# A two-layer convolution and feed-forward kernel: first h in two halves, new instruction orders, some PSUM copies on the other engine

## The chip, the cores and the metric

The kernel runs on one core of a Trainium2 chip. Five engines work side by side, each through its own queue in order: TensorE (PE, matrix products and transposes), VectorE (DVE), ScalarE (ACT), GpSimd (POOL) and SyncE (SP, which here only issues DMA transfers). PE writes to PSUM, and DVE or ACT has to copy a result from there to SBUF before PE can use it again. The metric is the device time of one execution in microseconds, lower is better, given as the median of several runs.

## What is computed

Two layers of the same two steps run over a sequence of 2048 rows of 512 channels in bfloat16. Step A is a long convolution (a short 4-tap convolution of k, times v, then convolved with a filter as long as the sequence, times the normalised input), step B a gated feed-forward block with 1792 hidden channels:

```python
def _A_ref(q, k, v, shift_k, ssm_k, ssm_D):
    ...
    for t in range(ks):
        k_shift = k_shift + k_pad[:, t:t + S, :] * shift_k[:, ks - 1 - t][None, None, :]
    kv = k_shift * v
    ...
    y = y + kv * ssm_D[None, None, :]      # y: kv convolved with ssm_k along the sequence
    return q * y

def _B_ref(x, w_gate, w_up, w_down):
    g = _silu(x @ w_gate)
    u = x @ w_up
    return (g * u) @ w_down

x = A_q
x = x + _A_ref(_layernorm(x, axis=-1), A_k, A_v, A_shift_k, A_ssm_k, A_ssm_D)
x = x + _B_ref(_layernorm(x, axis=-1), B_w_gate, B_w_up, B_w_down)
x = x + _A_ref(_layernorm(x, axis=-1), A_k, A_v, A_shift_k, A_ssm_k, A_ssm_D)
x = x + _B_ref(_layernorm(x, axis=-1), B_w_gate, B_w_up, B_w_down)
```

The convolution result y depends on k, v and the filter alone, so it is the same in both layers and is computed once.

## The kernel before

**Tiling.** The sequence is cut into four blocks c = 0..3 of 512 rows, a block into four residues r of 128 rows. The long convolution is done block by block in a spectrum: the filter's block (h, 512 channels by 512 positions, which has to be turned so that positions lie on partitions) and the block of kv go through small Fourier matrices (`fwd`), are multiplied on DVE (`product`, L665 to L679; block 0 in the form at L654 and L658) and come back through `inv`. Block 0 has its own code at the front; blocks 1 to 3 are spread among the feed-forward work.

**Units.** The feed-forward work comes in 16 units (layer, block, half), in the order block by block, in a block layer 0 half 0, layer 0 half 1, layer 1 half 0, layer 1 half 1. Before a unit, `prologue` takes the statistics of its two rows (bn_stats L821, bn_aggr L822, ve L824; or on ACT, L840 to L853), raises variance plus epsilon to the power -1/2 on POOL (`rstd`, L826 or L855: the power step), normalises (n or z, L879 on DVE, L874 on ACT), and, for the feed-forward input, turns z into zT with two DMA transposes on SP (L908). The first unit's z is turned on PE instead and copied from PSUM at L938 and L940. `gate_up` multiplies zT by the gate and up weights (PSUM tiles `pf`), ACT takes the silu of the one (sg, L974) and copies the other (ht, L977), DVE multiplies the two (L979); `down` multiplies ht by the last weights (PSUM tiles `pd`), ACT copies them (dn, L1075) and DVE adds them to x (L1078).

**The front.** SP issues h, k, v and q of block 0, then h and v of block 1 and the weights. PE turns h (`transpose_h`, L489, 16 transposes of 128 by 128, four to a residue), DVE or ACT copies them to hs (L499, L505; residue 0 with an addition, L502), PE multiplies by `fwd`, and the results are copied (`evacuate`, ev) and summed to G (L457, L459). `fwd` is made by DVE (index arithmetic `ph`), ACT (sine, L1145) and DVE again (the sign flips, L1151). k is turned on PE and copied to kTb (L384, L386); 16 diagonal matrices `dg` are built from the four taps (L1188, L1192) for the short convolution on PE (L522), whose result DVE multiplies by v (L536). Until the first h is there PE runs products of ones (`warm`, L1307), whose number `Plan.issue` works out from the planned starts.

**The order.** Every instruction is an entry of a list, made in program order by `plan.add` with its engine, a planned cost and what it reads and writes. The table ORDER (L55 to L113) holds for each entry its place in one global sequence; each engine's queue is that sequence cut down to the engine. The planned costs do not change the order: `Plan.order` uses them to choose which buffer of a ring a tile gets, and `issue` for the warming products. PW and PWA are the planned costs of the power step after DVE and ACT statistics.

Of the kernel before, what the change touches and what calls it, by code (L numbers as in the profile page):

```python
# [23 lines left out]
PW = 1.2  # L24
# [18 lines left out]
H_SPLIT = False  # L43
PWA = 2.4
EVEN = True
SUMS = False
K0 = "rows"
CK0, LT0 = 3.0, 3.5
# [5 lines left out]
SHARE = {(1, 0, 1): 2, (0, 2, 0): 2, (1, 3, 0): 2}  # L54
ORDER = [  # L55
# [57 lines left out]
]  # L113
R = 4
NZ = 3
# [1225 lines left out]
```

## Time and profile before

| | us |
|---|---|
| median of 3 runs (lowest, highest) | 343.08 (342.94, 343.32) |
| span of the profiled execution | 341.1 |
| PE busy | 336.9 (99%) |
| DVE busy | 282.4 (83%) |
| ACT busy | 252.5 (74%) |
| POOL busy | 37.3 (11%) |
| PE in the chain that ended last | 94% of the span |

The profile is one execution; its span runs from the first to the last instruction, and the runs' times contain what lies around the span. Busy shares are averages over stages: DVE and ACT are nearly full in the first hundred microseconds and have room at the end, so a stage's own row says more than the total. Rows in order of time give start, duration, engine, line, operation, written tile and what it reads, then in brackets the idle time of the engine before and what ended it; rows that name several instructions run together what follows closely on its engine. PE's products overlap: the next one starts before the former has left the array.

### The profile page before, as it was taken

To read this page: it belongs to the slowest core of one execution; us is meant where nothing else is said; L and a number is where in the kernel's file an instruction comes from. 1 tells how busy PE (TensorE), PEld (TensorE's weight loads), DVE (VectorE), ACT (ScalarE), POOL (GpSimd) and SP (SyncE) were. 2 spreads that over 40 slices of the span, in tenths; PEclk is the share of its full clock that TensorE was granted. 3 is DMA by queue.
4 is the path that set the end of the run, shared out by engine and by line. 5 is a ranking of instruction groups with operands and counts; after the bars stand their busy time and mean duration, and the time that the engine had idled before them with its cause. 6 is when DMAs were issued, how large, how long until landed. Compare 5 with 4: busy or idle time off the path is not lost.

```text
span 341.1 us, 6468 instructions
## 1 busy us (share of the span) xinstructions
PE 336.9 (99%) x2563; PEld 242.8 (71%) x2563; DVE 282.4 (83%) x478; ACT 252.5 (74%) x496; POOL 37.3 (11%) x46
## 2 busy tenths in 40 slices
PE   8999999999999999999999999999999999999996
PEld 7657858678687567768587756768685877777683
DVE  8899999999999999999999999889997533726022
ACT  7899999999977475778999973768665545545451
POOL 4000100002106100103100100101101000001000
PEclk9999999999999999999999999999999999999999
DMA  7999314050224175010110224010101110001111
GB/s 280 333 320 341 52 31 63 0 156 1 34 46 94 31 102 164 3 30 2 33 20 13 48 46 125 0 33 1 33 0 44 36 33 0 17 16 21 27 33 31
DMA packets 42088, 22.95 MB, mean 67 GB/s; under 512 B 33989, under 2 KB 39882, under 8 KB 42058
## 3 DMA queue, kind: packets, MB, share of 16 engines
q1 hardware_dynamic: 41904, 22.49, 26.0%
q8 instruction: 20, 0.33, 0.4%
q14 instruction: 10, 0.08, 0.1%
q10 hardware_dynamic: 154, 0.05, 0.1%
HBM read 12.33 MB, written 2.10 MB: 42 GB/s over the span
## 4 chain that ended last, share of the span: by engine, by line
PE 94%; ACT 3%; DMA 1%; SPq 0%; issue 0%; ACTq 0%
PE pf L323 57%; PE pd L994 28%; PE ps L323 6%; PE ps L470 2%; DMA kn<-in_A_k_dram 1%; ACT H L431 1%; ACT Yk L729 1%; ACT ks L526 0%; ACT n L874 0%; PE pt L378 0%; PE pt L489 0%; ACT zT L940 0%; ACT X L431 0%; SPq L354 0%; ACT xc L1052 0%
## 5 line engine op out<-in xcount | busy, mean ns | idle before, releaser
L323 PE MATMUL pf<-zT,wg_sb 128*128 128x256 bf16 (+1 forms) x872 | 110.3, 276 | 0.0
L323 PE MATMUL pf<-zT,wu_sb 128*128 128x256 bf16 (+1 forms) x872 | 110.0, 275 | 0.1
L994 PE MATMUL pd<-wd_sb,ht 128*128 128x512 bf16 (+1 forms) x462 | 106.2, 373 | 0.0
L323 PEld LDWEIGHTS <-wu_sb 128*128 128x128 bf16 x872 | 85.3, 98 | 18.9 <-issue 0.6
L323 PEld LDWEIGHTS <-wg_sb 128*128 128x128 bf16 x872 | 85.3, 98 | 17.3
L977 ACT CAST ht<-pf 128x512 bf16<-128x512 f32 x112 | 65.0, 592 | 23.0 <-PE pf L323 22.8
L974 ACT ACTIVATE sg<-pf 128x512 bf16<-128x512 f32 x112 | 66.6, 606 | 20.8 <-PE pf L323 17.3
L994 PEld LDWEIGHTS <-ht 128*128 128x128 bf16 x462 | 45.0, 98 | 44.1
L979 DVE TENSOR_TENSOR ht<-ht,sg 128x1024 bf16<-128x1024 bf16 (+1 forms) x61 | 38.9, 642 | 19.8 <-ACT ht L977 13.7
L826 POOL TENSOR_TENSOR rstd<-ve,nhalf 128x2 f32<-128x2 f32 x24 | 25.1, 1047 | 192.6 <-DVE ve L824 192.6
L821 DVE BATCH_NORM_STATS2 bnst<-xc 128x6 f32<-128x512 bf16 x48 | 31.8, 684 | 0.5
L1075 ACT CAST dn<-pd 128x512 bf16<-128x512 f32 x30 | 17.2, 590 | 17.5 <-PE pd L994 17.5
L431 ACT ACTIVATE X<-ps 128x512 bf16<-128x512 f32 x32 | 18.9, 606 | 10.5 <-PE ps L323 10.0
L1078 DVE TENSOR_TENSOR xc<-xc,dn 128x1024 bf16<-128x1024 bf16 x15 | 10.3, 687 | 16.8 <-ACT dn L1075 16.8
L669 DVE TENSOR_TENSOR t<-X,G 128x2048 bf16<-128x2048 bf16 x18 | 21.9, 1218 | 0.1
L665 DVE TENSOR_TENSOR t<-X,G 128x2048 bf16<-128x2048 bf16 x18 | 21.9, 1219 | 0.0
L855 POOL TENSOR_TENSOR rstd<-ve,nhalf 128x2 f32<-128x2 f32 x8 | 8.4, 1052 | 78.5 <-ACT ve L853 78.5
L679 DVE TENSOR_TENSOR Z<-Z,t 128x2048 bf16<-128x2048 bf16 x12 | 14.7, 1221 | 0.3
L677 DVE TENSOR_TENSOR t<-t,t 128x2048 bf16<-128x2048 bf16 x12 | 14.6, 1220 | 0.2
L431 ACT ACTIVATE H<-ps 128x512 bf16<-128x512 f32 x24 | 14.2, 612 | 0.0
L901 DVE TENSOR_TENSOR n<-n,Yk 128x1024 bf16<-128x1024 bf16 x15 | 10.3, 690 | 3.1 <-ACT n L874 1.9
L323 PE MATMUL ps<-hs,fwd 128*128 128x512 bf16 x40 | 12.7, 379 | 0.1
(103 smaller groups left out, 321.8 us busy)
## 6 DMA issues: line engine op xcount, KB each, us to landing
hn<-in_A_ssm_k_dram SPq DMA_DIRECT2D x4, 512.0 KB, 5.5
vt<-in_A_v_dram SPq DMA_DIRECT2D x4, 512.0 KB, 5.6
xc<-in_A_q_dram SPq DMA_DIRECT2D x4, 512.0 KB, 4.9
out_dram<-xc SPq DMA_DIRECT2D x15, 128.0 KB, 1.8
wg_sb<-in_B_w_gate_dram SPq DMA_DIRECT2D x1, 1792.0 KB
wu_sb<-in_B_w_up_dram SPq DMA_DIRECT2D x1, 1792.0 KB, 8.0
wd_sb<-in_B_w_down_dram SPq DMA_DIRECT2D x1, 1280.0 KB, 11.6
kn<-in_A_k_dram SPq DMA_DIRECT2D x1, 512.0 KB, 4.3
```

The lines of the kernel that those rows point to most:

```text
L323: nc.tensor.matmul(o, lhsT=lhsT, rhs=rhs, start=(n == 0), stop=(n == len(terms) - 1))
L431: add("ACT", act(D), lambda: nc.scalar.activation(out=view(), in_=ps.t[:], func=ACT.Copy, scale=scale), r=[ps], w=[(buf, keys)], conv=conv)
L665: dve(n * D, lambda t1=t1, part=part: nc.vector.tensor_mul(out=t1.t[:], in0=x.t[:, sl, 0, :], in1=g.t[:, sl, part, :]), [(x, key(slots, (0 ...
L669: dve(n * D, lambda t2=t2, part=part: nc.vector.tensor_mul(out=t2.t[:], in0=x.t[:, sl, 1, :], in1=g.t[:, sl, 1 - part, :]), [(x, key(slots ...
L679: dve(n * D, lambda t1=t1, part=part: nc.vector.tensor_add(out=z.t[:, sl, part, :], in0=z.t[:, sl, part, :], in1=t1.t[:]), [t1], [zk], con ...
L821: add("DVE", 0.6, lambda st=st, i=i: nc.vector.bn_stats(out=st.t[:], in_=xs[c].t[:, i, :]), r=[(xs[c], (i,))], w=[st])
L826: add("POOL", pw, lambda: nc.gpsimd.tensor_tensor(out=rstd.t[:], in0=ve.t[:], in1=nhalf.t[:].to_broadcast((P, n)), op=ALU.pow), r=[ve, nha ...
L974: add("ACT", act(D), lambda ps=ps, sl=sl: nc.scalar.activation(out=sg.t[:, sl], in_=ps.t[:], func=ACT.Silu), r=[ps], w=[(sg, (b,))], due=( ...
L977: add("ACT", act(D), lambda ps=ps, sl=sl: nc.scalar.copy(out=ht.t[:, sl], in_=ps.t[:]), r=[ps], w=[(ht, (b,))], due=(us[0], at, 1.5, "a"))
L979: dve(n * m * W, lambda: nc.vector.tensor_mul(out=ht.t[:], in0=ht.t[:], in1=sg.t[:]), [sg], [ht], due=(us[0], (k + n) / NF, 0.0, "h"))
L994: nc.tensor.matmul((pds[o] if not cs.start else pds[HP]).t[:, cs], lhsT=ht.t[:, q, at, o * P:(o + 1) * P], rhs=wt["d"].t[:, ft, cs], start ...
L1075: add("ACT", act(D), lambda o=o: nc.scalar.copy(out=dn.t[:, o, :], in_=pds[o].t[:]), r=[pds[o]], w=[(dn, (o,))], due=(unit, 1.0, 3.0, "h"))
```

## The change

1. **The first h in two halves** (H_SPLIT). SP issues two loads of 256 KB for block 0's h in place of one of 512 KB, and PE's transposes are cut into groups of two, one for each residue and half. The new table has the second half loaded first and PE's first entries in the order second half, first half of residue 0, then of residues 2, 1 and 3. The planned start of the first transposes makes 33 warming products ahead of them; before, there were 27 and 3 ahead of them, on both sides of the tap transposes, which now follow h.
2. **Copies from PSUM, and the dg builds, with an engine to choose.** They now go through `copy_out`, which has a form for ACT and one for DVE; `add` counts such entries in program order, and those whose number is in FLIP swap engines. Before the first feed-forward product: hs of residues 1 and 3 swap; one ev copy goes to ACT and two to DVE; two dg go to ACT and four to DVE; two kTb copies go to ACT and one to DVE; the zT copy of L940 goes to DVE. After it all go from ACT to DVE: the ht copies 76 in unit (0,0,1) and 171 in (1,1,1), the dn copy 148 of unit (1,1,0), the Yk copy 169, and from copy 211 on, an ht copy in (1,2,1), 14 ht copies and 6 dn copies. ACT's form of a plain copy is now an activation with Copy.
3. **A new ORDER** for all engines (1561 entries in place of 1556).
4. **Planned costs and latencies**: the power step 0.69 in place of 1.2 and 2.4 (0.85 for the first unit's), other waits between engines, and DMA transposes.
5. VFIRST and FIRST_ACT add branches that are not taken, or that keep what was there.

```diff
-PW = 1.2
+PW = 0.69
...
-H_SPLIT = False
-PWA = 2.4
+H_SPLIT = True
+PWA = 0.69
...
+FIRST_ACT = True
...
+VFIRST = False
...
+FLIP = {1, 2, 4, 11, 14, 15, 16, 17, 18, 24, 25, 26, 29, 31, 53, 76, 148, 169, 171, 211, 213, 214, 217, 218, 219, 220, 223, 224, 225, 231, 233, 235, 238, 239, 241, 242, 243, 245, 247}
 ORDER = [
-    0, 5, 1, 2, 3, 21, 16, 6, 14, 8, 15, 66, 69, 10, 7, 9, 4, 11, 34, 12, 17, 18, 13, 19, 20, 35, 26, 120, 121, 131, 27, 30, 31, 39, 37, 40, 36, 41,
...
+    1, 60, 6, 3, 2, 5, 11, 4, 10, 12, 0, 24, 26, 27, 15, 8, 9, 13, 16, 18, 20, 21, 22, 19, 28, 29, 30, 33, 51, 78, 127, 25, 23, 35, 17, 7, 31, 38,
...
-    SAME = {"PE": 0.0, "DVE": 0.12, "ACT": 0.05, "POOL": 0.1, "SP": 0.0}
-    CROSS = {"PE": 0.3, "DVE": 0.2, "ACT": 0.25, "POOL": 0.15, "SP": 0.0}
+    SAME = {"PE": 0.0, "DVE": 0.12, "ACT": 0.12, "POOL": 0.1, "SP": 0.0}
+    CROSS = {"PE": 0.2, "DVE": 0.14, "ACT": 0.15, "POOL": 0.05, "SP": 0.0}
...
         o = Op()
+        o.alt = None
+        if alt is not None:
+            here, there = (eng, cost, emit), alt
+            if self.choices in FLIP:
+                here, there = there, here
+            self.choices += 1
+            (eng, cost, emit), o.alt = here, there
...
+    def copy_out(dst, src, r, w, eng="ACT", n=None, scale=1.0, cost=None, **kw):
+
+        n = n or D
+        costs = dict(cost or {"ACT": act(n), "DVE": tt1(n)})
+        forms = {"ACT": lambda: nc.scalar.activation(out=dst(), in_=src(), func=ACT.Copy, scale=scale),
+                 "DVE": lambda: nc.vector.tensor_scalar(out=dst(), in0=src(), scalar1=scale, scalar2=None, op0=ALU.mult)}
+        other = "DVE" if eng == "ACT" else "ACT"
+        return add(eng, costs[eng], forms[eng], r=r, w=w, alt=(other, costs[other], forms[other]), **kw)
...
-                    add("ACT", act(D), lambda ps=ps, sl=sl: nc.scalar.copy(out=ht.t[:, sl], in_=ps.t[:]),
-                        r=[ps], w=[(ht, (b,))], due=(us[0], at, 1.5, "a"))
+                    copy_out(lambda sl=sl: ht.t[:, sl], lambda ps=ps: ps.t[:].rearrange("p (b m w) -> p b m w", b=per, m=m),
+                             [ps], [(ht, (b,))], due=(us[0], at, 1.5, "a"))
...
-                add("ACT", act(D), lambda o=o: nc.scalar.copy(out=dn.t[:, o, :], in_=pds[o].t[:]), r=[pds[o]], w=[(dn, (o,))],
-                    due=(unit, 1.0, 3.0, "h"))
+                copy_out(lambda o=o: dn.t[:, o, :], lambda o=o: pds[o].t[:], [pds[o]], [(dn, (o,))], due=(unit, 1.0, 3.0, "h"))
```

The other copies (hs, kTb, ev, Yk, zT) and the dg builds are put through the same choice in the same way. The first Y copy of block 0 gets an edge after the product before it, which places it behind that product in the sequence.

More of the change, by code (lines that the diff above doesn't have):

```diff
@@ L382, in transpose_k @@
             src = lambda pt=pt: pt.t[:].rearrange("d r p -> d p r")
-            if engs[dt % len(engs)] == "ACT":
-                add("ACT", 0.47, lambda src=src, dst=dst: nc.scalar.copy(out=dst(), in_=src()), r=[pt], w=[(kT[b], (dt,))])
-            else:
-                add("DVE", tt1(D), lambda src=src, dst=dst: nc.vector.tensor_copy(out=dst(), in_=src()), r=[pt],
-                    w=[(kT[b], (dt,))])
+            copy_out(dst, src, [pt], [(kT[b], (dt,))], engs[dt % len(engs)], cost={"ACT": 0.47, "DVE": tt1(D)})
         return k_in
@@ L391, in load_v @@
         vt[b] = new("y" if b == 1 else "v", "vt", [P, R, D], parts=R)
-        if b == 0 and K0 == "dma":
+        if b == 0 and K0 == "dma" and not VFIRST:
             return add("ACT", 0.45, lambda: nc.scalar.dma_start(out=vt[b].t[:], in_=v_t[:, b]), w=[vt[b]], lat=5.5, due=-69.5, after=[h0])
+        if b == 0 and VFIRST:
+            return add("SP", 0.5, lambda: nc.sync.dma_start(out=vt[b].t[:], in_=v_t[:, b]), w=[vt[b]], lat=LV0, due=due, after=after)
         return add("SP", 0.6, lambda: nc.sync.dma_start(out=vt[b].t[:], in_=v_t[:, b]), w=[vt[b]], lat=(6.6, 9.0)[b] if b < 2 else 5.5, due=due, after=after)
@@ L497, in transpose_h @@
             sl = slice(rows[0], rows[-1] + 1)
-            if engs[order.index(r0) % m] == "ACT":
-                add("ACT", act(len(rows) * D), lambda pt=pt, sl=sl: nc.scalar.copy(out=hs.t[:, sl, :], in_=pt.t[:]),
-                    r=[pt], w=[(hs, rows)], conv=conv)
-            elif row0 is not None and r0 == 0:
+            if row0 is not None and r0 == 0:
                 turns[0] = add("DVE", 0.335, lambda pt=pt: nc.vector.tensor_tensor(out=hs.t[:, 0, :], in0=pt.t[:, 0, :], in1=row0.t[:],
@@ L504, in transpose_h @@
             else:
-                turns[r0] = add("DVE", 0.335, lambda pt=pt, sl=sl: nc.vector.tensor_copy(out=hs.t[:, sl, :], in_=pt.t[:]),
-                    r=[pt], w=[(hs, rows)], conv=conv)
+                turns[r0] = copy_out(lambda sl=sl: hs.t[:, sl, :], lambda pt=pt: pt.t[:], [pt], [(hs, rows)], engs[order.index(r0) % m],
+                                     cost={"ACT": act(len(rows) * D), "DVE": tt2(len(rows) * D)}, conv=conv)
         return hs
@@ L724, with evacuate_y @@
     fresh = {}
-    def evacuate_y(k, rows):
+    def evacuate_y(k, rows, after=()):
         y, pss = Y[k], fresh[k]
         for r in rows:
-            add("ACT", act(D), lambda r=r: nc.scalar.activation(out=y.t[:, r, :], in_=pss[r].t[:], func=ACT.Copy, scale=2.0 if SUMS else 1.0),
-                r=[pss[r]], w=[(y, (r,))])
+            copy_out(lambda r=r: y.t[:, r, :], lambda r=r: pss[r].t[:], [pss[r]], [(y, (r,))], scale=2.0 if SUMS else 1.0, after=after)
     def inverse_rows(k):
@@ L886, in apply_norm @@
         rows = rows_of(h)
-        st = ln_stats_act(c, rows, after, (layer, c, h)) if on_act or ST1(layer, c, h) else ln_stats(c, rows)
-        nmr = shift_of(st, HP, due) if on_act or N_ACT(layer, c, h) else None
+        st = ln_stats_act(c, rows, after, (layer, c, h)) if on_act and FIRST_ACT or ST1(layer, c, h) else ln_stats(c, rows)
+        nmr = shift_of(st, HP, due) if on_act and FIRST_ACT or N_ACT(layer, c, h) else None
         n = new("n", "n", [P, HP, D], parts=HP)
@@ L936, in prologue @@
             pop = add("PE", pe(KD, P), go, r=[z, ident], w=[pt], due=-40)
-            if o:
-                add("DVE", 0.335, lambda pt=pt, o=o: nc.vector.tensor_copy(out=zT.t[:, :, o, :], in_=pt.t[:]), r=[pt], w=[(zT, (o,))], due=-45)
-            else:
-                add("ACT", act(D), lambda pt=pt, o=o: nc.scalar.copy(out=zT.t[:, :, o, :], in_=pt.t[:]), r=[pt], w=[(zT, (o,))], due=-45)
+            copy_out(lambda o=o: zT.t[:, :, o, :], lambda pt=pt: pt.t[:], [pt], [(zT, (o,))], "DVE" if o else "ACT",
+                     cost={"ACT": act(D), "DVE": tt2(D)}, due=-45)
             done = [zop, pop]
@@ L1111 @@
         h0 = load_h(0, "SP", -70)
-        k0 = load_k(0, -69.9, after=[h0])
+        if VFIRST:
+            v0 = load_v(0, -69.95, after=[h0])
+            k0 = load_k(0, -69.9, after=[v0])
+        else:
+            k0 = load_k(0, -69.9, after=[h0])
     elif K0 == "dma":
@@ L1132 @@
     ph = new("s8", "ph", [P, NS, P], I32, parts=NS)
-    v0 = load_v(0, -59, after=[k0, dr])
+    if not VFIRST:
+        v0 = load_v(0, -59, after=[k0, dr])
     x0 = load_x(0, -58, after=[v0, k0])
@@ L1186 @@
             w = [(dg, (dt * KS + j,))]
[L1187 to L1194 removed]
+            forms = {"ACT": (0.32, lambda j=j, dt=dt: nc.scalar.activation(out=dg.t[:, dt, j, :], in_=ident.t[:], func=ACT.Copy,
+                                                                            scale=tapF.t[:, dt, j:j + 1]))}
+            for e, q, cost in (("POOL", nc.gpsimd, 0.57), ("DVE", nc.vector, 0.163)):
+                forms[e] = (cost, lambda j=j, dt=dt, q=q: q.tensor_scalar(out=dg.t[:, dt, j, :], in0=ident.t[:],
+                                                                          scalar1=tapF.t[:, dt, j:j + 1], scalar2=None, op0=ALU.mult))
+            e = {"D": "DVE", "A": "ACT", "P": "POOL"}[DGE[dt]]
+            other = {"DVE": "ACT", "ACT": "DVE", "POOL": "DVE"}[e]
+            add(e, *forms[e], r=[ident, tapF], w=w, alt=(other, *forms[other]))
     k_in = transpose_k(0, "pc", eng(KTE)) if K0 == "rows" else k0
```

47 lines of the change are left out of this document (17 added, 30 removed), and 115 rows, old and new, of the table ORDER.

## The prediction

> **What bounds the kernel now.** I read the busy time by stage first, then TensorE (PE) in order of time, then the front of VectorE (DVE), then who waits for whom. Busy time of each engine in stretches cut at the events that matter (stretch, its length, then PE, weight loads, DVE, ScalarE (ACT), POOL, clock, DMA share, GB/s):
>
> ```profile
> 4.35:32.23 27.88, 27.42 (x260) 17.87 (x261) 26.20 (x60) 26.41 (x57) 4.72 (x7) 1.00 1.06 343
> 32.23:338.10 305.87, 305.87 (x2269) 221.70 (x2268) 252.88 (x406) 223.86 (x437) 31.62 (x30) 1.00 0.19 40
> 32.23:242.00 209.77, 209.76 (x1549) 151.56 (x1549) 203.75 (x314) 173.92 (x346) 25.24 (x22) 1.00 0.23 49
> 242.00:262.00 20.00, 20.00 (x149) 14.47 (x148) 18.12 (x28) 12.22 (x23) 1.92 (x2) 1.00 0.07 14
> ```
>
> From 32.23 us, the first feed-forward product, to 338.1 PE is never idle, at the full granted clock. Its work is fixed, so the end can only move by (a) the time of that first product and (b) stalls that the new orders bring after it. DVE is the close second: 203.75 of 209.77 us up to 242, and it has room only after 262: 252.88 - 203.75 - 18.12 = 31.0 us busy in the 76.1 left. The first product waits for the front. PE, ACT and DVE rows there:
>
> ```profile
> 0.76 3.04 PE L1307 MATMUL wm<-const-bfloat16-1.0 128*128 128x128 bf16 x27 [0.76 <-PEq L1325]
> ...
> 4.35 1.06 PE L489 MATMUL pt<-ident,hn 128*128 128x128 bf16 x16
> ...
> 32.23 1.91 PE L323 MATMUL pf<-zT,wu_sb 128*128 128x256 bf16 x16
> ```
>
> ```profile
> 3.90 0.63 ACT L1145 ACTIVATE fwd<-ph 128x512 bf16<-128x512 int32 x1 [0.81 <-DVE ph L1143]
> ...
> 10.44 0.69 DVE L536 TENSOR_TENSOR vt<-ps,vt 128x512 bf16<-128x512 f32 x1 [0.96 <-PE ps L323]
> ...
> 29.61 0.76 DVE L527 TENSOR_TENSOR vt<-ks,vt 128x512 bf16<-128x512 bf16 x2 [0.24 <-ACT ks L526]
> ...
> 31.28 0.42 DVE L938 COPY zT<-ptz 128x512 bf16<-128x512 bf16 x1
> ...
> 31.57 0.62 ACT L940 COPY zT<-ptz 128x512 bf16<-128x512 bf16 x1
> ```
>
> The first product starts as the second zT copy ends (31.57 + 0.62 = 32.19). Upstream of it DVE has hardly a pause but the 0.96 and 0.24 us shown.
>
> **h in two halves.** Removed: one load; added: two, on SP's queue ahead of k, v and q, so those are issued about one issue later; 16 transposes become 8 groups of 2 with the same matmuls. How the transfer landed:
>
> ```profile
> 0.72 0.46 SPq L354 DMA_DIRECT2D hn<-in_A_ssm_k_dram  x1
> DMA to landing us min/median/max: 3.6/5.5/7.5
> ```
>
> The first issue is the 3.6 us one: 0.72 + 3.6 = 4.3, the 4.35 of the first transpose. Half of the bytes can land between 0.72 + 1.8 = 2.5 (all of it proportional to bytes) and 4.3; the other half no earlier than today's 4.3. In the new table PE's first entries are the second half of row 0, then its first half, so PE goes on after only 2 of 16 transposes: at 1.06/16 = 0.07 us each, 0.13 us. The transposes of the tap weights, now done at 3.7 while PE waits, move behind them and cost about that again. Taken: 0. The 33 warming matmuls stand where 27 in a row and a few later ones stood; at the 3.04/27 = 0.11 us of today's they fill 3.7 us from 0.76 and end at 4.5 at the latest, 0.2 after h is whole, and at 4.1 if the last ones run at the 0.07 of the transposes: 0, with 0.2 as the other end.
>
> **The front of DVE.** Copies and diagonal builds that change engine before 32 us, with their prices:
>
> ```profile
> L434 DVE TENSOR_SCALAR ev<-ps 128x512 bf16<-128x512 f32 x2 | 1.4, 688 | 0.0
> L386 DVE COPY kTb<-pt 128x512 bf16<-128x512 bf16 x2 | 1.4, 690 | 0.1
> L1192 DVE TENSOR_SCALAR dg<-ident,tapF 128x128 bf16<-128x128 bf16 x8 | 2.0, 266 | 0.1
> ```
>
> ```profile
> 36.74 2.35 DVE L593 TENSOR_TENSOR G<-H,G 128x2048 bf16<-128x2048 bf16 x2
> ```
>
> Two 1.22 us products take 2.35, so neighbours overlap by 0.08 and a 0.69 costs the queue 0.61. DVE gets two diagonals more (4 come, 2 go: +0.53), one ev copy (2 come, 1 goes: +0.61), one kTb copy fewer (1 comes, 2 go: -0.61), hs one for one: +0.53 ahead of the first zT copy. In return two sums of G now stand ahead of the vt product that waited 0.96 for PE; that wait is covered. But both sign flips (L1151) now stand ahead of DVE's first hs copy, and the later one needs the second sine on ACT: DVE is done with its index work at 3.9, the sine ends at 3.90 + 0.63 = 4.53, so about 0.45 is lost that is filled with diagonals today; behind the later flip stand DVE's hs copies, and PE's first products wait for these. 0.53 - 0.96 + 0.45 = 0. The second zT copy, moved from ACT to DVE, follows the first: 31.28 + 0.34 + 0.42 = 32.04 in place of 32.19. Taken for the first product: 0. Ends: -0.7 without the new wait (0.53 - 0.96 - 0.15 = -0.6, rounded outward), +0.8 if the 0.96 stays.
>
> **DVE from 32 to 262 us.** Summing the durations over the two tables, DVE's work ahead of the normalise for the second row of unit (1,2,1) is 4.95 us more: 0.86 of it lies before the first product (the 0.53 and a zT copy, 0.33); two ht copies and one dn copy come from ACT (3 x 0.61 = 1.83); the statistics of the other rows (1.13) and one 2048-wide product (1.14) have been moved ahead of it. PE has 0.43 more ahead of its first product there. What slack that unit has, and what DVE waits for up to 242:
>
> ```profile
> 239.68 2.51 SPq L908 DMA_TRANSPOSE zT<-z  x2
> ```
>
> ```profile
> 244.38 0.49 PE L323 MATMUL pf<-zT,wu_sb 128*128 128x256 bf16 x3
> ```
>
> ```profile
> zT<-z SPq DMA_TRANSPOSE x30, 2.5
> ```
>
> ```profile
> DVE ht L979 <- ACT ht L977: 1.0, 3, 0.6
> DVE n L879 <- POOL rstd L826: 0.9, 1, 0.9
> DVE xc L1078 <- ACT dn L1075: 0.6, 1, 0.6
> DVE m L552 <- ACT X L431: 0.3, 1, 0.3
> DVE ka L620 <- ACT ka L616: 0.3, 1, 0.3
> DVE n L901 <- ACT Yk L703: 0.2, 1, 0.2
> DVE ht L979 <- ACT sg L974: 0.2, 1, 0.2
> ```
>
> The second transfer is issued 1.25 after 239.68 and lands 2.5 later, at 243.4: slack 0.95. A later DVE meets fewer waits, at best all 3.5 us of them. Some waits for the power stay, see next: 1.6. So 4.95 - 0.86 - 0.43 - 0.95 - (3.5 - 1.6) = 0.8 us by which that row is late. Behind that normalise stand DVE's products for the ht of the unit before; PE stands still for 0.8 and its whole queue with it. The end below nothing (every wait vanishes, 0.8 - 1.6 < 0) is 0, since PE has no idle time to give back; the other end, no wait vanishes, is 0.8 + 1.9 = 2.7. After 262 DVE has over half its time free, and the 20 more copies there (12 us) are hidden by that; without it they would cost up to 12. The planner's other new costs and latencies, and the edge from the first Y copy to the product before it, choose only slots of buffers and the number of warming matmuls, as the order is a table: 0, hidden as long as no slot is asked for early. ACT only gets lighter; its copy is now of the form of the silu, a few ns longer, hidden by ACT's free time.
>
> **The power step.** The planner's cost goes from 1.2 and 2.4 us to 0.69. The rows:
>
> ```profile
> L826 POOL TENSOR_TENSOR rstd<-ve,nhalf x24: 687/695/6210, 29.4 to 310.9; 128x2 f32<-128x2 f32 x24
> ```
>
> ```profile
> 310.62 0.68 DVE L979 TENSOR_TENSOR ht<-ht,sg 128x1024 bf16<-128x1024 bf16 x1
> 311.89 0.41 DVE L879 TENSOR_SCALAR z<-xc,mv,rstd 128x512 bf16<-128x512 bf16 x1 [0.58 <-POOL rstd L826]
> ```
>
> ```profile
> 310.86 1.00 POOL L826 TENSOR_TENSOR rstd<-ve,nhalf 128x2 f32<-128x2 f32 x1 [5.40 <-DVE ve L824]
> ```
>
> ```profile
> 110.00 1.22 DVE L669 TENSOR_TENSOR t<-X,G 128x2048 bf16<-128x2048 bf16 x1
> ```
>
> ```profile
> 105.56 6.21 POOL L826 TENSOR_TENSOR rstd<-ve,nhalf 128x2 f32<-128x2 f32 x1 [11.57 <-DVE ve L824]
> ```
>
> 0.69 is the undisturbed power. Begun inside a DVE product it ends 0.55 after that product: 311.86 against 311.30. Once it found no pause in seven instructions and ended at 111.77, 0.55 after the one that ended at 111.22. So with one product between statistics and normalise, DVE waits 0.58, and with none 0.87 (the 0.9 row). In the new DVE order up to 242 one power has none behind it (0.9) and two have too little (a 1.22 product and a short step: 0.4; a 0.69 product and a normalise: 0.3). That is the 1.6.
>
> [...]
>
> **Sum.** 341.1 of span + 0 (front) + 0.8 (unit (1,2,1)) = 341.9. The three runs' median, 343.08, lies 1.98 above this execution's span: 343.9 us.
>
> **Rivals.** A, all of DVE's later work is swallowed: the 3.5 us of waits vanish, the 1.6 for the power too, because what stands after it can go first; PE stays gapless and the front is even: 343.1. For it: slack of the other units; against it: the 0.9 row recurs in the new order. B, the other side: the front gains. If the second sine is not late for DVE, -0.6, and if the 0.24 before the vt product of block 1 goes too, -0.84, kept only if every later DVE margin holds: 342.2. It decides where the first normalised rows are copied; against it are the 4.95. C, the power starves: eleven powers of the new order up to 242 have two to eight DVE instructions between statistics and reader. Where such a one misses all pauses the reader waits 0.58; four of these are 2.3 us on a DVE that has no slack left: 343.9 + 2.3 = 346.2.
>
> **How the numbers follow.** A measurement of this kernel tells 0.2%, 0.69 us, from no change: faster is below 342.4, slower above 343.8. Forecast 0.47, with 343.5 to 345 its own range and 0.38 of it above 343.8; A 0.18; B 0.18, 0.16 of it below 342.4; C 0.17, all of it slower. Faster 0.16, within 0.29, slower 0.55. The range 342.2 to 346 takes in the front's ends (-0.7, +0.8) about the forecast and most of B and C.
>
> **What would show it.** First feed-forward product at 32.2 within 0.5; the first transposes no more than 0.15 earlier; DVE's wait at the first vt product gone and one before its first hs copy in its place; PE no longer filled from 32 to 338, its holes between 160 and 262, before products on zT, ht or Z and released by DVE; DVE's waits for the power over 0.9 up to 242. I am wrong if PE is gapless there, if its holes come before 100 us, or if ACT, a DMA or the last 80 us set them.

## The result and the profile after

| | before | after |
|---|---|---|
| median of 4 runs (lowest, highest), us | 343.2 (342.94, 343.42) | 345.5 (345.4, 345.72) |
| span of the profiled execution, us | 341.1 | 343.9 |
| first feed-forward product, us | 32.23 | 32.72 |
| idle time of PE from there to its end, us | 0 | 2.14 |

The changed kernel takes 1.0069 times as long, 95% interval 1.0055 to 1.0083: slower by 2.3 us. In the experiments four of e1's six runs, three of e8's four and one of e4's twelve were granted 0.995 of TensorE's clock; e1's four are 1.3 us longer (346.98 to 347.35), and its two at the full clock are the ones compared below.

Busy time by stage of the changed kernel (stretch, its length, then PE, weight loads, DVE, ACT, POOL, clock, DMA share, GB/s):

```profile
4.34:32.72 28.38, 27.74 (x264) 18.23 (x264) 26.04 (x62) 25.27 (x53) 4.49 (x7) 1.00 1.10 309
32.72:60.25 27.53, 27.53 (x220) 21.32 (x219) 27.46 (x38) 26.91 (x61) 3.55 (x3) 1.00 0.38 97
60.25:66.00 5.75, 4.11 (x29) 2.57 (x27) 3.21 (x5) 3.16 (x7) 2.55 (x1) 1.00 0.11 22
66.00:340.80 274.80, 274.78 (x2027) 197.62 (x2024) 234.52 (x389) 181.67 (x348) 31.92 (x27) 1.00 0.16 39
```

From its first feed-forward product on PE is gapless but in one stretch of 5.75 us, and there DVE and ACT are idle for nearly half of the time too: no engine is overloaded, each waits for another. A hole of PE is counted here from the start of the last product ahead of it to the next start, less the 0.11 us (256 columns) or 0.22 (512) at which products follow each other elsewhere; by that count PE stands still for 1.14 at 60.35, 0.73 at 64.53 and 0.27 at 65.47, 2.14 us in all. With the front that is 0.49 + 2.14 = 2.63 of the 2.8 us by which the span grew.

**The front.** PE's rows:

```profile
0.76 3.68 PE L1320 MATMUL wm<-const-bfloat16-1.0 128*128 128x128 bf16 x33 [0.76 <-PEq L1338]
4.59 0.38 PE L505 MATMUL pt<-ident,hn 128*128 128x128 bf16 x2
5.13 1.30 PE L505 MATMUL pt<-ident,hn 128*128 128x128 bf16 x14 [0.16 <-DMA hn<-in_A_ssm_k_dram]
6.36 0.29 PE L1186 MATMUL pt<-ident,tapR 4*128 4x4 bf16 x4
...
32.72 1.03 PE L337 MATMUL pf<-zT,wg_sb 128*128 128x256 bf16 x8
```

After the first two transposes PE waits for the other half, and h is whole only at about 5.1, where the single load was there by 4.35. The 14 transposes behind the pause take 0.09 us each, the 16 of before 0.07. That is TensorE's clock: the trace's records of the granted clock begin, at full, at 5.87 us here and at 3.73 in the kernel before, and transposes start every 0.107 us ahead of that moment and every 0.056 behind it. From the first start behind the pause to the last it is 1.08 us where the full clock would give 13 x 0.056 = 0.73. So h is turned at 5.13 + 1.30 = 6.43 in place of 5.41, 1.02 later, 0.35 of it by the clock, and the first feed-forward product follows 26.29 us after that in place of 26.82. The new order of the front is 0.53 us shorter, and in this execution the later load and the later clock take back twice that.

**The stretch at 60 us.** ACT's copies that prepare the turned filter of block 2, the DMA transposes that read all four of them, and PE's product that needs the last transpose; first after, then before:

```profile
49.38 1.24 ACT L616 COPY hr<-hn 128x512 bf16<-128x512 bf16 x2
...
52.15 0.66 ACT L616 COPY hr<-hn 128x512 bf16<-128x512 bf16 x1
...
53.19 0.67 ACT L616 COPY hr<-hn 128x512 bf16<-128x512 bf16 x1
...
53.89 6.35 SPq L620 DMA_TRANSPOSE hs<-hr  x4
...
61.49 0.38 PE L337 MATMUL ps<-hs,fwd 128*128 128x512 bf16 x1 [0.97 <-DMA hs<-hr]
```

```profile
49.72 1.82 ACT L603 COPY hr<-hn 128x512 bf16<-128x512 bf16 x3
...
51.56 6.19 SPq L607 DMA_TRANSPOSE hs<-hr  x4
```

The new table has two copies of dn and one of ka between the copies hr. The last hr ends 2.32 us later (53.86 against 51.54; 0.49 of it is the later front), the transposes go out 2.33 later, and PE, which could have begun its product at 60.35, begins it at 61.49: the first hole, 1.14. Before, it had no wait at all.

The second hole has another cause. The power after ACT's statistics, and what ACT, DVE and PE do around it:

```profile
59.20 3.60 POOL L866 TENSOR_TENSOR rstd<-ve,nhalf 128x2 f32<-128x2 f32 x1 [11.96 <-ACT ve L864]
...
58.17 1.22 DVE L678 TENSOR_TENSOR t<-X,G 128x2048 bf16<-128x2048 bf16 x1
59.30 1.22 DVE L682 TENSOR_TENSOR t<-X,G 128x2048 bf16<-128x2048 bf16 x1
60.44 0.69 DVE L988 TENSOR_TENSOR ht<-ht,sg 128x1024 bf16<-128x1024 bf16 x1
61.04 1.22 DVE L690 TENSOR_TENSOR t<-t,t 128x2048 bf16<-128x2048 bf16 x1
...
62.84 0.48 ACT L878 ACTIVATE nmr<-sm,rstd 128x1 f32<-128x1 f32 x2 [2.74 <-POOL rstd L866]
63.22 1.50 ACT L885 ACTIVATE n<-xc,nmr,rstd 128x512 bf16<-128x512 bf16 x2
64.63 0.57 ACT L445 ACTIVATE H<-ps 128x512 bf16<-128x512 f32 x1
...
65.26 0.38 PE L337 MATMUL ps<-hs,fwd 128*128 128x512 bf16 x1 [0.57 <-ACT H L445]
```

```profile
58.97 0.88 POOL L855 TENSOR_TENSOR rstd<-ve,nhalf 128x2 f32<-128x2 f32 x1 [12.84 <-ACT ve L853]
...
58.09 1.22 DVE L665 TENSOR_TENSOR t<-X,G 128x2048 bf16<-128x2048 bf16 x1
59.34 1.23 DVE L677 TENSOR_TENSOR t<-t,t 128x2048 bf16<-128x2048 bf16 x1
```

After (first fence), four two-input products on DVE run into each other, each starting 0.08 to 0.09 before the end of the one ahead. The power begins in the first and ends at 62.80, 0.54 after the end of the fourth. ACT's nmr needs it and waits 2.74 us with everything queued behind it, the copy H among it, which PE needs at 64.53. Before (second fence), the product behind the first read what the first had written and started 0.03 after its end; that was pause enough, and the power took 0.88.

### The profile page after: what moved, and what is told of

It is laid out like the page before. It is cut to its first block, busy times and chain, and to the rows that moved or that the text cites. A ratio compares the mean times of both kernels' runs of the same rounds, so it can differ in the third digit from the quotient of the medians.

```text
span 343.9 us, 6484 instructions
## 1 busy us (share of the span) xinstructions
PE 337.7 (98%) x2564; PEld 243.2 (71%) x2564; DVE 294.9 (86%) x505; ACT 239.5 (70%) x469; POOL 43.6 (13%) x46
## 4 chain that ended last, share of the span: by engine, by line
PE 84%; DVE 7%; ACT 5%; DMA 1%; POOL 1%; issue 1%; SPq 0%; DVEq 0%; ACTq 0%
PE pf L337 51%; PE pd L1003 26%; PE ps L337 6%; DVE t L667 1%; DMA hn<-in_A_ssm_k_dram 1%; POOL rstd L866 1%; ACT sg L983 1%; DVE Z L671 1%; PE ps L820 1%; DVE m L565 1%; DVE G L606 1%; ACT hr L616 1%; ACT ht L445 1%; ACT X L445 0%; ACT n L885 0%
## 5 line engine op out<-in xcount | busy, mean ns | idle before, releaser
L337 PE MATMUL pf<-zT,wg_sb 128*128 128x256 bf16 x872 | 110.3, 275 | 0.0
L983 ACT ACTIVATE sg<-pf 128x512 bf16<-128x512 f32 x112 | 65.5, 603 | 40.0 <-PE pf L337 33.8
L445 ACT ACTIVATE ht<-pf 128x512 bf16<-128x512 f32 x96 | 56.6, 603 | 24.7 <-PE pf L337 24.3
L837 POOL TENSOR_TENSOR rstd<-ve,nhalf 128x2 f32<-128x2 f32 x24 | 29.6, 1233 | 220.5 <-DVE ve L835 220.1
L445 ACT ACTIVATE dn<-pd 128x512 bf16<-128x512 f32 x23 | 13.7, 606 | 19.9 <-PE pd L1003 19.8
L446 DVE TENSOR_SCALAR ht<-pf 128x512 bf16<-128x512 f32 x16 | 10.9, 686 | 13.9 <-PE pf L337 13.7
L866 POOL TENSOR_TENSOR rstd<-ve,nhalf 128x2 f32<-128x2 f32 x8 | 10.5, 1318 | 44.7 <-ACT ve L864 44.7
L690 DVE TENSOR_TENSOR t<-t,t 128x2048 bf16<-128x2048 bf16 x12 | 14.6, 1219 | 0.1
```

What stands on the lines that cost most here:

```text
L337: nc.tensor.matmul(o, lhsT=lhsT, rhs=rhs, start=(n == 0), stop=(n == len(terms) - 1))
L445: forms = {"ACT": lambda: nc.scalar.activation(out=dst(), in_=src(), func=ACT.Copy, scale=scale), "DVE": lambda: nc.vector.tensor_scalar(o ...
L690: dve(n * D, lambda t1=t1, t2=t2, comb=comb: nc.vector.tensor_tensor(out=t1.t[:], in0=t1.t[:], in1=t2.t[:], op=comb), [t2], [t1], conv=conv)
L837: add("POOL", pw, lambda: nc.gpsimd.tensor_tensor(out=rstd.t[:], in0=ve.t[:], in1=nhalf.t[:].to_broadcast((P, n)), op=ALU.pow), r=[ve, nha ...
L866: add("POOL", PWA, lambda: nc.gpsimd.tensor_tensor(out=rstd.t[:], in0=ve.t[:], in1=nhalf.t[:].to_broadcast((P, n)), op=ALU.pow), r=[ve, nh ...
L983: add("ACT", act(D), lambda ps=ps, sl=sl: nc.scalar.activation(out=sg.t[:, sl], in_=ps.t[:], func=ACT.Silu), r=[ps], w=[(sg, (b,))], due=( ...
```

## The experiments

Each is an edit to the changed kernel. `placed` rewrites the table: the entries named first go, in that order, directly ahead of the entry named last. Medians stand in us, beside 29 runs of the kernel before on the same chip in each series (343.19, 343.25 and 343.35).

| | edit | median | over before, 95% interval | first product, us | holes of PE after it, us |
|---|---|---|---|---|---|
| e1 | copies hr ahead | 345.7 (2 at full clock) | 1.0095 (1.0070 to 1.0119), all six | 32.83 | 1.87, 0.27 |
| e2 | short copy on DVE | 344.25 | 1.0025 (1.0010 to 1.0039) | 32.30 | 1.03 |
| e3 | both | 343.51 | 1.0005 (0.9989 to 1.0021) | 32.51 | none |
| e4 | h in one load | 345.17 | 1.0072 (1.0046 to 1.0099) | 32.34 | 0.70, 1.18, 0.27 |
| e5 | e1 and products swapped | 343.84 | 1.0014 (1.0000 to 1.0028) | 31.91 | 0.27 |
| e6 | e3 and e4 | 343.08 | 0.9987 (0.9972 to 1.0003) | 32.11 | none |
| e7 | e6, 29 warming products | 343.04 | 0.9992 (0.9971 to 1.0014) | 34.48 | none |
| e8 | e3, 24 short copies | 347.98 | 1.0127 (1.0100 to 1.0154) | 32.88 | 2.96 |
| e9 | e1, nmr and n later on ACT | 345.66 | 1.0065 (1.0051 to 1.0079) | 32.88 | 0.94, 0.39, 0.61 |
| e10 | e6, k first | 343.36 | 0.9992 (0.9976 to 1.0007) | 32.58 | none |
| e11 | e6, k in the middle | 343.07 | 0.9990 (0.9978 to 1.0002) | 32.14 | none |
| e12 | e6 again | 343.06 | 0.9993 (0.9983 to 1.0003) | 32.97 | none |

### Two holes, each in the other's shadow (e1 to e3)

**e1**, the copies hr together and ka behind the copies dn:

```diff
-        plan.issue(*plan.order(ORDER), 32.0, warm)
+        plan.issue(*plan.order(placed(ORDER, MOVES)), 32.0, warm)
+
+MOVES = (((546, 543), 576), ((576,), 286))
...
```

> The four ScalarE copies that feed the DMA transposes of block 2's filter stand together again; the copy of ka and the two copies dn go behind them. They should end near 52.1 us in place of 53.9, so the last transpose lands near 59.8 and TensorE no longer waits at 60.25 (1.14 us). Theory 'two holes, one in the shadow of the other': ScalarE still stands until 62.8 behind the power that POOL cannot begin, its H copy still ends near 65.2, and TensorE waits for that instead: the time stays at 345.5 +- 0.3. Rival 'two holes that add up': 1.1 us less, 344.4. Rival 'the power has nothing to do with it, the late transposes are all of it': 2.1 less, 343.4.

PE's rows of e1 where the two holes were:

```profile
60.47 0.38 PE L337 MATMUL ps<-hs,fwd 128*128 128x512 bf16 x1
...
62.65 1.03 PE L1003 MATMUL pd<-wd_sb,ht 128*128 128x512 bf16 x4
65.38 0.38 PE L337 MATMUL ps<-hs,fwd 128*128 128x512 bf16 x1 [1.70 <-ACT H L445]
```

The wait for the DMA is gone, and PE comes 1.0 us earlier to the next spectrum product, which waits for the same copy H; that copy ends when the power lets it. The holes sum to 1.87 + 0.27 = 2.14, to the hundredth what they were, and the time is unchanged (345.63 and 345.81). The rivals (1.1 and 2.1 less) fall.

**e2**, one short copy with one input between the first two of the four products; **e3** has it together with the edit of e1:

```diff
+    tick = const.tile([P, 1], F32, name="tick", tag="tick")
+    for n in (302,):
+        o = plan.ops[n]
+
+        def go(emit=o.emit):
+            nc.vector.tensor_copy(out=tick[:], in_=nhalf.t[:])
+            emit()
+        o.emit = go
```

> A copy of 128x1 on VectorE, one input, between the two 1.22 us products at 59.3 us. If a short instruction with one input lets POOL's power begin, that power ends near 60.0 in place of 62.8, ScalarE's wait of 2.7 us falls to about 0.1, and the holes at 64.3 and 65.3 (0.73 and 0.27) go: 1.0 less, 344.5; the hole at 60.25 (1.14) stays. Rival 'the power is not what ScalarE's lateness costs': no change, 345.5. Rival 'a short copy does not open the gap': the power still takes over 2 us and nothing changes.

> Both edits. Theory 'two holes in each other's shadow': both go, TensorE is gapless from 32.7 on but for the 0.7 us that the kernel before has too: 2.1 less, 343.4. Rival 'VectorE is late anyway' (the step of the prediction): the 2.1 us that TensorE no longer stands at 60 us come back in part before the first product of unit (1,2,1), whose rows then land up to 1.0 late, at about 246.3 against a need at 245.3: 344.4, with a hole at 245.

DVE, POOL and ACT of e3 at that place:

```profile
57.95 1.22 DVE L678 TENSOR_TENSOR t<-X,G 128x2048 bf16<-128x2048 bf16 x1
59.09 0.14 DVE L1327 COPY tick<-nhalf 128x1 f32<-128x1 f32 x1
59.15 1.21 DVE L682 TENSOR_TENSOR t<-X,G 128x2048 bf16<-128x2048 bf16 x1
...
59.00 0.72 POOL L866 TENSOR_TENSOR rstd<-ve,nhalf 128x2 f32<-128x2 f32 x1 [11.96 <-ACT ve L864]
...
59.76 0.49 ACT L878 ACTIVATE nmr<-sm,rstd 128x1 f32<-128x1 f32 x2
```

An instruction that takes 0.06 us of DVE's queue brings the power from 3.60 to 0.72 and ACT's wait from 2.74 to nothing. In e2 the first hole stays, 1.03, and the second is gone: 344.25. With both edits PE is gapless from its first product to its end, 343.51, and no hole comes back at 245 us: the rival of e3 falls. So removing either cause alone is worth 0 or some 1.2, and both together 2.0.

### What opens the queue for the power (e5), and what carries its lateness (e9)

**e5** adds nothing: the sum t L690 goes directly behind the products it reads, ahead of the product of ht.

```diff
+MOVES = (((546, 543), 576), ((576,), 286), ((403,), 382))
```

> The late copies of the turned filter mended as in the first run; and no instruction is added on VectorE: the sum of the two 1.22 us products at 58 to 60 us is put directly behind them, ahead of the product of ht. It reads what the product before it writes, so it cannot overlap its end. Theory 'a power begins where VectorE's queue has a pause, however short': the pause of some 0.03 us at 60.4 lets the power in, it ends near 61.0 in place of 62.8 and no hole is left: 343.5, as with the short copy. Rival 'what let the power in was the one-input copy itself': the power still ends near 62.8 and a hole of 2.1 us stays at 63 to 66: 345.6.

DVE, POOL and ACT of e5:

```profile
58.49 1.22 DVE L682 TENSOR_TENSOR t<-X,G 128x2048 bf16<-128x2048 bf16 x1
59.74 1.23 DVE L690 TENSOR_TENSOR t<-t,t 128x2048 bf16<-128x2048 bf16 x1
...
58.39 1.86 POOL L866 TENSOR_TENSOR rstd<-ve,nhalf 128x2 f32<-128x2 f32 x1 [11.96 <-ACT ve L864]
...
60.29 0.48 ACT L878 ACTIVATE nmr<-sm,rstd 128x1 f32<-128x1 f32 x2 [1.00 <-POOL rstd L866]
```

The sum starts 0.03 after the end of the product it reads (59.71) where the product of ht started 0.08 before it. The power ends at 60.25, 0.54 after that pause. So a pause of 0.03 us is enough, without any copy. In e3 DVE has no pause at that place (its rows overlap), so there it was the copy that let the power in; whether by its one input or by being short is not separated. ACT's wait falls to 1.00 and one hole of 0.27 stays; 343.84, against the 343.5 expected. In the changed kernel the power missed the ends of three two-input products in a row (59.39, 60.52 and 61.13) and ended 0.54 after the end of the fourth (62.26), behind which DVE stood 2.50.

**e9** leaves the power late and puts what needs it further back in ACT's queue:

```diff
+MOVES = (((546, 543), 576), ((576,), 286), ((378, 379, 380, 381, 382, 383), 386))
```

> The copies of the filter ahead as in the first run, no short copy: the power still finds no pause and ends near 62.8. But ScalarE's four instructions that need it (nmr and the normalise, two each) are put behind its next H copy and ht copy. Theory 'the power reached TensorE only because it stood at the head of ScalarE's queue': the H copy runs at about 62 and no hole is left on TensorE at 60 to 66; VectorE's product on n waits about 1 us longer, which its later slack takes: 343.5 to 344. Rival 'it reaches TensorE through VectorE anyway': a hole of 1 to 2 us comes later than 66: 344.6 to 345.6.

The power still takes 3.60. The copy H runs at 60.93 and the wait for it is gone, but holes of 0.94, 0.39 and 0.61 come in its place:

```profile
65.08 0.69 DVE L912 TENSOR_TENSOR n<-n,Yk 128x1024 bf16<-128x1024 bf16 x1 [2.66 <-ACT n L885]
...
65.58 1.03 PE L337 MATMUL pf<-zT,wg_sb 128*128 128x256 bf16 x8 [0.77 <-ACT sg L983]
...
74.26 1.03 PE L337 MATMUL pf<-zT,wu_sb 128*128 128x256 bf16 x8 [0.44 <-DMA zT<-z]
```

My theory falls here, and the rival is half right. ACT still stands 0.67 and 1.15 us, now waiting for PE, then has the four moved instructions (2 us) ahead of the silu that PE needs: that is the hole of 0.94. DVE stands 2.66 us for the normalised n, and what follows in its queue is late: a product for ht, which PE needs (0.39), and the row of x, up to its transposes (0.61). So the late power reaches PE on two roads, through ACT's queue and through DVE's, and moving four instructions back on ACT closes neither.

### The front (e4, e6, e7, e10 to e12)

**e4** loads h in one piece and leaves the cut transposes and all orders:

```diff
-                o = add(eng, 0.5, lambda sl=sl: q.dma_start(out=hn[b].t[:, sl], in_=h3[:, sl, 0:L]), w=[(hn[b], (n,))],
+                o = add(eng, 0.5, lambda n=n: n and q.dma_start(out=hn[b].t[:], in_=h3[:, :, 0:L]), w=[(hn[b], (n,))],
```

> Only the load of the first h is one transfer of 512 KB again, and k, v and q are issued half a microsecond earlier; the cut transposes and all orders stay. First theory: the second half landing at 5.0 in place of 4.3 is what makes the first feed-forward product 0.49 late, so that product comes at 32.2 again; but the filter's copies and transposes at 50 to 60 us hang on ScalarE, which is full from 4 to 54, so what the front gains is gained at the end only if ScalarE's queue moves with it: 345.0 if so, 345.5 with a hole at 60 us grown by 0.5 if not. Rival: the new orders of the front are to blame, not the landing: first product still at 32.7.

The first product comes at 32.34, and the holes at 60 us are 0.70 + 1.18 + 0.27 = 2.15 as before; 345.17 is not told apart from the 345.5 of the change (two of its twelve runs, of which no trace is kept, are at 348.6 and 349.0). The holes did not grow, so ACT's queue moved with the front, and the profile's span is 343.5 in place of 343.9, by as much as the first product is earlier. **e6** has the same edit together with those of e3, **e12** is e6 once more:

> The copies of the filter ahead, the short copy, and the first h in one transfer, with k issued 0.5 us earlier. With no hole left at 60 us to take the front's gain, the end should follow the first feed-forward product. Theory 'the split costs the front': h is whole at about 4.4 and k long there, first product near 32.3 at the latest, as the 33 warming products hold TensorE until 4.4 to 4.6: 343.3 with a narrow spread. Rival 'the split costs nothing': as without it, 343.5.

> The version with the three edits once more, beside the two that move k: level with the kernel before within 0.2 per cent, at 343.1 +- 0.3, the first feed-forward product at 32.1 to 32.4 in the profile and no hole on TensorE after it.

343.08 and 343.06 against 343.51 in e3: the medians put the cost of the halves at some 0.4 us, but the three intervals overlap, so that cost is not shown. Without the halves and without the holes the new orders are level with the kernel before (0.9987 and 0.9993, both intervals with 1 in them). The front of e6, of e12, and k's first transposes in e3:

```profile
4.73 1.08 PE L505 MATMUL pt<-ident,hn 128*128 128x128 bf16 x16 [0.29 <-DMA hn<-in_A_ssm_k_dram]
5.75 0.29 PE L1186 MATMUL pt<-ident,tapR 4*128 4x4 bf16 x4
```

```profile
4.91 1.76 PE L505 MATMUL pt<-ident,hn 128*128 128x128 bf16 x16 [0.47 <-DMA hn<-in_A_ssm_k_dram]
6.60 0.29 PE L1186 MATMUL pt<-ident,tapR 4*128 4x4 bf16 x4
```

```profile
7.67 0.84 PE L392 MATMUL pt<-ident,kn 128*128 128x128 bf16 x12 [0.41 <-DMA kn<-in_A_k_dram]
```

From the tap transposes to the first feed-forward product it is 32.11 - 5.75 = 26.36 in e6, 32.97 - 6.60 = 26.37 in e12, and 32.72 - 6.36 = 26.36 in the changed kernel: where k is there in time, the front is a fixed chain behind h's last transpose. That transpose moved by 0.9 us between two executions of one kernel, and e12's profile is not the 32.1 to 32.4 that I expected. The load is 0.18 of it (4.73 and 4.91), most of the rest is the clock, whose records begin at 4.54 in e6 and at 6.39 in e12. Over the twelve profiles with 33 warming products they begin at 3.78 to 6.40 with the halves (seven) and at 4.54 to 6.39 with one load (five). So the first product of one profile, the changed kernel's +0.49 among them, says little about the halves.

What the halves do is seen at k. Its load is issued 0.50 later (1.74 in place of 1.24), and issue and time to landing together put it at 6.5 to 7.9 us in the seven profiles with the halves, at 5.5 to 6.1 in the seven with one load. In e2 and e3, whose clock rose at 3.8, PE waits for it (the last row above), and the first product comes 24.84 after k's first transpose: in e3 26.95 behind the taps, 0.59 more than the chain of h alone. In e6 k no longer holds PE up.

**e7** caps the warming products, **e10** and **e11** turn three quarters of k earlier:

```diff
-        for _ in range(n):
+        for _ in range(min(n, 29)):
```

```diff
+MOVES = (((546, 543), 576), ((576,), 286), ((70, 74, 72), 122), ((71, 73), 125))
```

(e11 has 124 in place of 122; in e10 the plan also puts three warming products ahead of k.)

> The same with 29 warming products in place of 33, so that they end before h is whole. In five traces so far the first feed-forward product comes 24.83 us after the first transpose of k, and with these orders that transpose waits for h's transposes and five spectrum products. Theory: h's transposes at 4.35, k's at 7.1, first product at 31.9, end 0.3 before that of the kernel before: 342.9. Rival 'from there VectorE, not k, sets the first product': 343.3 as with 33.

> On top of the version that was level with the kernel before or a little faster (343.08): TensorE turns three quarters of k ahead of its first six spectrum products, and ScalarE copies two kTb ahead of its first ev. Theory 'the front follows k': k's transposes at 6.0 in place of 7.3, first feed-forward product up to 1.3 earlier, 341.8 to 342.8. Rival 'the spectrum products, 0.8 later, then hold VectorE and ScalarE up by as much': no gain or a loss, 343.0 to 343.9.

> The same with k's transposes behind the first two spectrum products instead of ahead of them: half of the step. By the first theory half of the gain (342.4 to 342.9), by the rival none (343.0 to 343.5).

All three leave the median where it was (343.04, 343.36, 343.07). In e10 and e11 k's transposes begin at 6.46 and 6.45 in place of 7.27, and the first product at 32.58 and 32.14 is no earlier than the 32.11 of e6: with one load k is not what the front waits for. The constant distance that it had kept in five traces was in three of them k running behind h, and in e2 and e3 k's own late load. e7 is the worse bargain: 8 of its runs lie at 342.56 to 343.32, but 4 at 344.54 to 345.34, where all 24 runs of e6 and e12 are below 343.9 (e3, also with 33 warming products, has one at 345.37). Its profile caught one of the four:

```profile
4.57 1.90 PE L505 MATMUL pt<-ident,hn 128*128 128x128 bf16 x16 [0.55 <-DMA hn<-in_A_ssm_k_dram]
```

Its clock records begin only at 10.17; the 16 transposes take 1.90 in place of 1.08, and the first product comes at 34.48. That the last four warming products are cover against that is an estimate from these counts of runs; of the other runs no trace is kept.

### The step that the prediction had priced (e8)

**e8** puts 24 short copies on DVE ahead of the entry at 223 us:

```diff
-    for n in (302,):
+    for n, times in ((302, 1), (1004, 24)):
```

> The copies of the filter ahead and the short copy as before, and 24 short copies (0.06 to 0.15 us each, 1.4 to 3.6 us in all) on VectorE at 223 us, ahead of the second normalise of unit (1,2,1). That row now lands 1.1 us before TensorE needs it. Theory 'the 1.1 us are the cover and VectorE's queue is otherwise full': the row is late by what is added less 1.1 and at most 1.1 more that its waits for the power can swallow; TensorE gets a hole of that size at about 245 us, which is the stall that the prediction had put there. Rival 'VectorE hangs on TensorE and catches up': no hole, 343.5.

They took more than I had taken them for:

```profile
223.69 4.46 DVE L1328 COPY tick<-nhalf 128x1 f32<-128x1 f32 x24
...
237.14 0.29 ACT L878 ACTIVATE nmr<-sm,rstd 128x1 f32<-128x1 f32 x1 [4.83 <-POOL rstd L866]
...
237.97 2.45 PE L337 MATMUL pf<-zT,wg_sb 128*128 128x256 bf16 x13 [2.79 <-ACT sg L983]
```

4.4 us more of DVE, close to the 4.95 of the prediction, cost 347.98 - 343.51 = 4.5 us in the medians. Not all of that is waiting. The profile's span is 5.0 longer than e3's (346.5 and 341.5): 0.37 is the later first product, 2.96 the hole, and some 1.7 comes behind the hole, where the clock fell (the last row of this text) and 16 products started every 0.213 us in place of 0.109. So of the 4.4 some 1.4 were taken up before they reached PE, within the 1.1 to 2.2 expected. The hole is not at 245, before the unit's first product, but at 234.9, and it comes through POOL and ACT: the late statistics on DVE hold POOL's queue up, a power behind them is late for ACT's nmr, and the silu behind that is late for PE. The cover that I had counted, at the transfer of z, is not the first to give way.

## Why the prediction was right, and where it was wrong

The time fell in the range and on the side that the prediction held likeliest, 0.5 above its own range for the likeliest case and nearer to the third rival's 346.2 than to the forecast's 343.9. The mechanism was another: the 0.8 that the sum had added did not come, and 2.14 came where it had nothing. As far as that sum goes, the number is right by luck.

**"ACT only gets lighter": the step that failed.** It was made from what the flips take away, not from ACT's order, and ACT's free time was an average of the whole. From 32.23 to 60 us ACT was busy for 27.53 of 27.77 us before the change:

```profile
32.23:60.00 27.77, 27.77 (x220) 21.51 (x220) 27.60 (x38) 27.53 (x61) 3.06 (x3) 1.00 0.38 62
```

There a copy that is put three places further back is late by what was put before it, and the transposes on SP with it: the last hr ends 21.14 us after the first feed-forward product, where it was 19.31 before and is 19.51 in e1, so 1.6 of the 2.32 are these three copies. The hole of 1.14 follows from it; mending it is worth nothing alone (e1) and some 0.7 in the medians once the other cause is mended (e2 and e3: 344.25 and 343.51). The prediction asked of each moved step what queue it passed, and did not ask it of ACT.

**The power step: right in kind, wrong in place and price.** The third rival had eleven powers that could miss all pauses, each at 0.58, with DVE as the reader. Three did (3.60, 3.73 and 5.00 us), and the two later ones cost nothing. The one that cost had ACT as its reader, at the head of a full queue: 2.74 us of ACT, 1.0 of PE beside the first hole, 2.14 without it (e1).

**DVE up to 262 us: 4.95 us that were not there.** No stall came at 244 us, and none came when the holes at 60 were mended (e3). DVE's busy time from the first feed-forward product to the second normalise of unit (1,2,1), before, after and in e3:

```profile
32.23:239.53 207.30, 207.29 (x1534) 150.09 (x1534) 201.28 (x310) 172.11 (x343) 25.24 (x22) 1.00 0.23 49
```

```profile
32.72:243.51 210.79, 209.15 (x1541) 150.58 (x1540) 202.97 (x318) 172.56 (x346) 33.78 (x24) 1.00 0.22 53
```

```profile
32.51:241.12 208.61, 207.52 (x1520) 150.46 (x1540) 202.88 (x320) 172.68 (x346) 30.89 (x24) 1.00 0.22 54
```

4.95 - 0.86 = 4.09 should have been added; 202.97 - 201.28 = 1.69 was. The prediction summed durations, and in DVE's queue here a duration costs its length less the 0.08 by which the next instruction starts early, or plus some 0.03 where that one reads what it wrote. Counted over the rows of DVE in these stretches, neighbours overlap at 233 of 309 places before and at 277 of 317 after. The new order puts other work between an instruction and its reader, and that paid for most of the copies: the overlaps add up to some 3.4 us more than before. It is the same thing that starved the power: fewer pauses. The second term was wrong too. The 0.95 of cover was measured from SP's second issue, which stood behind the first; the normalises themselves were done 1.0 earlier:

```profile
239.20 0.73 DVE L879 TENSOR_SCALAR z<-xc,sm,rstd 128x512 bf16<-128x512 bf16 x2
```

So in e3 the second row comes 208.61 - 207.30 = 1.31 later after the first product than before, with 0.95 + 1.0 of cover and PE 0.43 later: nothing is late. What real work costs there, e8 shows: of 4.4 us 2.96 reached PE, and the clock that fell behind the hole added some 1.7.

**The front: taken as 0, measured +0.49 in the profile.** The waits came as foretold: the one at the first vt product is gone, and DVE waits 0.53 for the second sine and 1.21 before its first copy of hs. Two terms were off. The other half's landing, "no earlier than today's 4.3" and taken at that, was 5.1, beyond the 0.2 kept as the other end. And the prediction had seen that k would be issued one issue later but gave that no price: k landed at 6.5 to 7.9 in place of 5.5, and in e2 and e3 it set the first product. The clock's later rise, 0.35 of the 1.02 by which h was late, varies between executions with and without the halves. The gain of the new order there, 0.53, is near the 0.6 of the second rival. What the halves cost in all, some 0.4 by e3 and e6, is not clear of noise.

**What was to show it.** The first product within 0.5 of 32.2 and the changed waits at the front: right. The first transposes no more than 0.15 earlier: they were 0.24 later. DVE's waits for the power over 0.9 up to 242: right, 2.2 (three before n, 1.9 together, and 0.3 before z). Holes between 160 and 262, released by DVE: wrong; the text named holes before 100 us and ACT or a DMA as what would prove it wrong, and all three came. The first rival, in which DVE's later work is swallowed, was right about DVE.

## What to carry to other kernels

Ask of every queue in turn, in the stage and not over the whole, what stands ahead of an instruction that another engine waits for: a full queue off the critical path pays for each exchange in it (here ACT, busy for 27.53 of 27.77 us, where three copies put between the copies hr cost 1.6 us). Two holes in a row can hide each other, so undo both before either is called harmless. A queue made denser by spacing readers from writers takes its pauses from whoever lived in them; a short one-input copy, or a reader directly behind its writer, at the right place lets them in again (here the power, 3.60 us, took 0.72 in e3 with the copy and 1.86 in e5 with the reader). And the front of one profile is one draw of the moment at which the clock rises (3.78 to 6.40 us in twelve profiles with 33 warming products): compare several.

## What the runs showed of the hardware

A power on POOL that begins under two-input products on DVE, or 0.08 us ahead of the first (the one at 82.84), did not always go in at the next end of one. Two more powers of the changed kernel:

```profile
82.84 3.73 POOL L837 TENSOR_TENSOR rstd<-ve,nhalf 128x2 f32<-128x2 f32 x1 [0.62 <-DVE ve L835]
...
110.71 5.00 POOL L837 TENSOR_TENSOR rstd<-ve,nhalf 128x2 f32<-128x2 f32 x1 [13.34 <-DVE ve L835]
```

With the one at 59.20 they are five to seven times the 0.69 of an undisturbed one, and a pause of 0.03 us (e5) or a copy of 128x1 (e3) was enough to let it in.

TensorE's pace at the start goes by the granted clock, and the moment of its rise differs from execution to execution. The trace records each change (ahead of the first record the clock column of a stretch shows 1.00 and cannot be used). In all fourteen profiles the transposes of h start every 0.106 to 0.108 us ahead of the first record and every 0.055 to 0.057 behind it, the first few and those next to a pause or to the record itself apart: the 16 transposes of h took 1.08 in e6 (record at 4.54), 1.76 in e12 (6.39) and 1.90 in e7 (10.17). After the hole of 2.96 us in e8 the clock fell:

```profile
237.90:242.00 4.10, 4.03 (x22) 2.90 (x22) 4.10 (x7) 3.92 (x12) 0.00 (x0) 0.58 0.00 0
```

By the records it fell at 238.51, 0.54 us after PE had begun again, and rose 3.41 us later. The stretches at full clock are 337.92 us long in eleven profiles and 334.51 in e7 and e12, 3.41 less; in e8 the three stretches together are 341.33, 3.41 more. So in these traces these lengths lie steps of 3.41 us apart, and e8's fall lasted one. One such step at half clock (products every 0.213 us in place of 0.109) is a mean of 0.995 over e8's 346.5 us; four of e1's six runs have the same mean, but whether its hole of 1.87 brought that on is not shown, as its profile is of a run at the full clock.

The first record, at full clock, came 3.0 to 5.6 us after PE's first product at 0.76 in thirteen profiles, and 9.4 after it in e7. The 29 warming products of e7 fill 3.25 us, 33 fill 3.44 to 3.68. Four of e7's twelve runs were long (344.54 to 345.34); why the other eight were not is not shown.
